# A new order table for a block-sparse attention fused with a gated feed-forward: other engines and buffers for many pieces, three more pairs of score banks, 42 unread products instead of 102

## The chip, the cores and the metric

The kernel runs on one core of a Trainium2 chip. The metric is the device time of that core in microseconds (us). The engines are PE (matrix products; its loading of weights is shown as PEld), DVE (vector), ACT (activations), POOL, also called GpSimd, and SP, which here only issues DMA transfers. [...]

## The reference

Four batches of eight heads, 768 positions and 64 dimensions. Each block of 32 queries sees the blocks beside it, the first and the last block of the sequence, and three sampled blocks; the first and the last block of queries see everything. The result of the attention goes through a gated feed-forward.

```python
batch, n_heads, seq, head_dim = (4, 8, 768, 64)
scores = scale * np.matmul(q, k.transpose(0, 1, 3, 2))
mask = np.abs(blk_i - blk_j) <= window
mask = mask | (blk_i == 0) | (blk_j == 0) | (blk_i == n_blocks - 1) | (blk_j == n_blocks - 1)
# and the three sampled blocks of each block of queries
attn = softmax(np.where(mask, scores, -1e9)); x = np.matmul(attn, v)
gate = 1.0 / (1.0 + np.exp(-(x @ w_gate)))     # 512 -> 1536
return (gate * (x @ w_val)) @ w_out            # 1536 -> 512
```

## The kernel before

The work is cut into 1446 named pieces, each some instructions on one engine. A table, ORDER, lists them in one row: for each piece its name, its engine (P, A, D, G, S for PE, ACT, DVE, GpSimd and SP), the number of each buffer that it takes, and after a plus sign how many unread products of 128x512 (tile WZ, line 1083) PE does ahead of it. `Planner.run` walks the table and the pieces are issued in that order, so every engine's queue is a part of the table. The lines that set it:

```python
item, _, idle = item.partition("+")
name, _, how = item.partition(":")
o.eng, o.idle = self.ENG[how[0]], int(idle or 0)
...
for o in pl.run(ORDER):
    for _ in range(o.idle):
        pin(nc.tensor.matmul(banks[7], WZ[:, 0:128], WZ, start=True, stop=True))
```

The names in the table, with the batch first (`sl0_81` is batch 0, the step that begins with block 8, half 1):

- `ldk`, `ldq`, `ldv`: the loads of a batch (DMA issued by GpSimd, line 417). `trk`, `trq`, `evk`, `evq`: transposition of K and Q on PE and its copy out of PSUM (tiles KT and QT). `vsh`: V put into another order (line 587, tile XL or stg). `scr`: V written back to DRAM. `w`: a window of four blocks of V read from there into V1, `vg`: the three sampled blocks of V of one block read into V2 (SP, line 745), `vfl`: the first and last block copied in (line 641).
- Each batch has eleven steps of two blocks. `kw` copies the window of K (line 728), `kg` gathers three sampled blocks of K for each of two blocks on GpSimd (line 712, six copies), `kfl` the fixed ones. `sc`: scores on PE into a pair of banks (lines 784 and 773); `mx`: row maxima on DVE (line 796); `ex`: exponentials with sums on ACT, one piece for each half of the heads (line 806, tile P, three buffers); `rz`: reciprocal of the sums (line 815); `sl`: the multiplication of P with it, one piece for each half, on ACT (line 828, two instructions), DVE (line 830, two instructions) or GpSimd (line 824, one instruction); `tp`: transposition on PE (line 842); `te`: copy out of PSUM (line 848, tile PTS, three buffers); `pv`: product with V (line 860); `xe`: copy into the feed-forward's input (lines 887 and 889, tiles XT and XL).
- `dsc`, `dmx`, `dex`, `dsl`, `dtp`, `dte`, `dpv`, `dxe` are the same for the first and the last block of queries, which see all keys (lines 916 to 996).
- The feed-forward works on nine groups of rows (128 rows in groups 0 and 1, 256 in 2 to 4, 512 in 5 to 8) and twelve slices of the width 1536: `pg` and `pu`: the gate's and the value's products (line 1029), `th`: tanh on ACT (line 1038), `h`: the gating on DVE (line 1043, tile HT), then for each 128 rows `py`: the output product (line 1060, twelve products), `ys`: copy (DVE line 1067, ACT line 1069), `st`: store.

Banks: scores take a pair out of banks 0, 1 and 2; banks 3 and 4 take the transpositions and the attention's products; banks 5, 6 and 7 take the feed-forward's products (group 0 has 5 and 6 alone, the last two groups take all eight). The first four steps may also have the pair of banks 5 and 6. The pairs come from one line:

```python
spool = duo((0, 1), (1, 2), (0, 2), *TUNE["sx"])
```

Of the kernel before, what the change touches and what calls it, by code (L numbers as in the profile page):

```python
# [17 lines left out]
B, H, S, D = 4, 8, 768, 64  # L18
# [27 lines left out]
 'sx': [],  # L46
# [10 lines left out]
vg0_5:S dte0_00:D regPOOL0_1:G ex0_60:A2 dtp0_01:P0+4 vg0_7:S rz0_4:D sl0_41:D ex0_61:A sc0_8:P0 sc0_10:P3 kw0_14:D2
sl0_40:A rz0_6:D mx0_8:D7 vg0_4:S kw0_12:A1 tp0_4:P11+3 dte0_01:A mx0_10:D1 kg0_12:G vg0_6:S sl0_60:A dpv0_0:P0+4
w0_8:G0 sl0_61:D ex0_80:A1 te0_4:D wv1:G vg0_8:S ex0_81:A sc0_12:P2+2 tp0_6:P10 kw0_18:G1 ex0_100:A0 vg0_11:S
kg0_14:G te0_6:D ex0_101:A mx0_12:D0 pv0_4:P1+3 wg2:G vg0_9:S kg0_18:G rz0_8:D rz0_10:D ex0_120:A2 xe0_4:D dxe0_0:D  # L60
vg0_10:S sl0_100:A sl0_80:G pv0_6:P0+8 sl0_101:A sc0_14:P0 wv2:G xe0_6:D kw0_2:A2 sl0_81:D w0_12:G0 pg0_0:P00+2
pu0_0:P1 th0_0:A0 tp0_10:P12 h0_0:D kw0_16:D0 pg0_1:P10 regSP0_1:S mx0_14:D1 pu0_1:P0 kg0_16:G th0_1:A2 tp0_8:P00
ex0_121:A pg0_2:P10 h0_1:D wo0:G te0_10:D pu0_2:P0+1 th0_2:A2 ex0_140:A0 pg0_3:P10 vg0_13:S h0_2:D regPOOL0_2:G
rz0_12:D sl0_120:D pu0_3:P0 th0_3:A0 sl0_121:A pg0_4:P10+1 h0_3:D te0_8:D pu0_4:P0 th0_4:A2 vg0_12:S ex0_141:A
sc0_16:P2 h0_4:D pg0_5:P10 mx0_16:D5 pv0_8:P1 kw0_20:A0 pu0_5:P0 w0_16:S0 tp0_12:P00 th0_5:A1 kg0_20:G ex0_160:A1
h0_5:D vg0_15:S rz0_14:D sl0_141:D pg0_6:P00+1 pu0_6:P1 te0_12:D th0_6:A0 w0_2:G0 xe0_8:A sc0_18:P0 h0_6:D pg0_7:P00
mx0_18:D4 pu0_7:P1 ex0_161:A pv0_10:P0 vg0_14:S wo1:G th0_7:A1 ex0_180:A2 h0_7:D pg0_8:P00+2 rz0_16:D xe0_10:D
kg0_2:G th0_8:A2 vg0_19:S sl0_160:D pu0_8:P0+3 pg0_9:P10 kw0_1:G1 sl0_161:D sc0_2:P2 h0_8:D th0_9:A1 ex0_181:A wo2:G
pu0_9:P0 mx0_2:D7 vg0_18:S pg0_10:P10 tp0_16:P02 kg0_1:G th0_10:A0 pu0_10:P1 h0_9:D ex0_20:A1 pg0_11:P00 h0_10:D
sl0_140:G vg0_16:S pu0_11:P1 th0_11:A1 ex0_21:A sc0_20:P0+1 h0_11:D vfl0A:G pg1_0:P10 mx0_20:D3 pu1_0:P0 th1_0:A0  # L70
pg1_1:P20 pu1_1:P1 th1_1:A2 tp0_14:P11 te0_16:A h1_0:D h1_1:D pg1_2:P00 rz0_18:D sl0_181:D pu1_2:P1 ldv10:G0
vg0_17:S pg1_3:P20 th1_2:A2 rz0_2:D pv0_12:P0 h1_2:D th1_3:A0 sl0_20:G pu1_3:P2 xe0_12:A pg1_4:P10 h1_3:D te0_14:D
regSP0_2:S pu1_4:P2 w0_1:G0 th1_4:A0 ex0_200:A0 pg1_5:P10 h1_4:D sl0_180:D pu1_5:P0 pg1_6:P20 sl0_21:D th1_5:A2
pv0_14:P0 th1_6:A0 h1_5:D ldk10:G1 pu1_6:P2 vg0_3:S xe0_14:A pg1_7:P10 h1_6:D pu1_7:P0 ldq10:G2 pg1_8:P20 th1_7:A2
sc0_1:P2 h1_7:D th1_8:A0 vfl0B:G ex0_201:A pu1_8:P1 vg0_21:S mx0_1:D2 pg1_9:P00 tp0_18:P10 th1_9:A2 pu1_9:P2
pg1_10:P00 h1_8:D rz0_20:D tp0_2:P01 h1_9:D vg0_20:S th1_10:A0 sl0_201:D ex0_10:A2 pu1_10:P2 pg1_11:P10 h1_10:D
pu1_11:P2 th1_11:A0 sl0_200:A dsc0_23:P02 h1_11:D ex0_11:A py1_0:P2 dmx0_231:D1 vg0_2:S rz0_1:D dmx0_230:D4
dex0_231:A0 dex0_230:A1 dsl0_231:D py0_0:P1 sl0_11:D te0_2:A ys1_0:D0 dsl0_230:D te0_18:A vsh1:D3 dtp0_230:P00
# [12 lines left out]
sc1_6:P0 ys2_0:A1 py2_1:P1 kg1_8:G rz1_20:D mx1_6:D3 te1_2:A st2_0:S vg1_20:S kw1_10:G0 sl1_201:A sl1_200:D ldq20:G0
rz1_4:D h3_0:D ex1_60:A1 sl1_40:D kg1_10:G regSP1_0:S pg3_1:P20 ex1_61:A sc1_8:P2 pv1_1:P1 mx1_8:D7 kw1_12:G1
ys2_1:A0 tp1_20:P02 regPOOL1_1:G th3_1:A2 pu3_1:P1 sl1_41:A w1_4:S0 rz1_6:D te1_20:D pg3_2:P20 ex1_80:A2 vg1_7:S
pu3_2:P0 xe1_1:D tp1_4:P00 th3_2:A1 sl1_60:G ex1_81:A sc1_10:P0 h3_1:D vg1_6:S h3_2:D pg3_3:P10 mx1_10:D5 kg1_12:G
te1_4:A pu3_3:P0 pg3_4:P20 th3_3:A2 vg1_4:S kw1_14:G0 pv1_2:P0 th3_4:A0 h3_3:D ex1_100:A0 kg1_14:G pu3_4:P1 xe1_2:D
pg3_5:P00 pu3_5:P2 rz1_8:D h3_4:D th3_5:A2 sl1_61:A sc1_12:P2 h3_5:D pg3_6:P10 kw1_16:G1 mx1_12:D0 ex1_101:A
tp1_6:P11 vg1_5:S pu3_6:P0 th3_6:A2 sl1_81:D ex1_120:A1 pg3_7:P10 h3_6:D pv1_20:P0 rz1_10:D te1_6:D sl1_101:G
th3_7:A0 pu3_7:P2 w1_8:S0 xe1_20:A dsc1_0:P02 h3_7:D vg1_11:S sl1_80:G ex1_121:A dmx1_01:D1 pg3_8:P20 th3_8:A2
kg1_16:G dmx1_00:D2 dex1_01:A0 pu3_8:P2 scr2:S tp1_8:P12 h3_8:D dex1_00:A1 pg3_9:P10 dsl1_01:D pu3_9:P2 th3_9:A0
dsl1_00:D te1_8:A dsc1_23:P02 h3_9:D dtp1_00:P00 dmx1_231:D7 dtp1_01:P1 vg1_8:S pg3_10:P20 dte1_00:D dex1_231:A0  # L100
dte1_01:D pv1_4:P0 th3_10:A2 pu3_10:P0 dmx1_230:D1 vg1_9:S xe1_4:A dpv1_0:P1 sl1_100:D dex1_230:A1 h3_10:D
tp1_10:P00 vg1_10:S rz1_12:D pg3_11:P20 dxe1_0:A dsl1_230:D pu3_11:P1 te1_10:A dsl1_231:D dtp1_230:P10 w2_2:S0
sc1_14:P0 th3_11:A0 dte1_230:D dtp1_231:P0 kw1_18:G0 h3_11:D pv1_6:P1 kg1_18:G mx1_14:D4 dte1_231:A py3_0:P1
w1_12:S0 xe1_6:A gv2:S sl1_121:D ex1_140:A0 st2_1:S regSP1_1:S ex1_141:A dpv1_23:P1 ys3_0:A1 rz1_14:D pv1_8:P0
dxe1_23:D rrq2:G3 sc1_16:P2 vg1_13:S pg4_0:P10 mx1_16:D1 pv1_10:P1 th4_0:A2 py3_1:P2 sl1_120:A sl1_140:G vg1_14:S
xe1_10:D ex1_160:A2 sl1_141:G xe1_8:A st3_0:S ex1_161:A w1_16:S0 pu4_0:P0 vg1_19:S trk201:P1 h4_0:D pg4_1:P10
# [1009 lines left out]
```

## Time and profile before

| | |
|---|---|
| median of 3 runs | 339.71 us (338.84 to 340.23) |
| span of the profiled execution, first to last instruction | 336.5 us |
| the profiled execution's own time | not among the times listed; the median is 3.2 us above the span |
| busy: PE, DVE, ACT, GpSimd | 318.1, 230.8, 232.4, 128.1 us |
| unread products (line 1083) | 102, busy 28.5 us |
| DMA | 43.14 MB, mean 128 GB/s |

An engine's busy time is the union of its instructions, whose ends are modelled on PE, so a busy PE is not at its peak. "x4" behind a row stands for four instructions. What stands in square brackets behind a row is the idle time ahead of it and the engine that ended it. The granted clock is a share of TensorE's full clock.

### The profile page before, as it was taken

What the parts mean: (1) busy time and instruction counts of PE and PEld (TensorE: products, weight loads), DVE (VectorE), ACT (ScalarE), POOL (GpSimd) and SP (SyncE); (2) the same over time, 40 slices, a digit from 0 to 9 for tenths busy, and PEclk for the clock granted to TensorE, in tenths of its full rate; (3) what the DMA queues carried; (4) which work ended last, traced back from release to release, by engine and by line L of the source; (5) the groups of instructions that cost most, each with busy time, mean ns of one, the idle gap of its engine ahead of it and who ended that gap; (6) DMA issues with size and microseconds to landing.
All of it is one profiled execution on the core that took longest, in us unless ns stands there. A gap on an engine that the chain in (4) does not pass through costs nothing.

```text
span 336.5 us, 11685 instructions
## 1 busy us (share of the span) xinstructions
PE 318.1 (95%) x4230; PEld 194.5 (58%) x4230; DVE 230.8 (69%) x493; ACT 232.4 (69%) x663; POOL 128.1 (38%) x376
## 2 busy tenths in 40 slices
PE   8999887899999789999998999999999999999995
PEld 3545565748776667796555655555645555554442
DVE  3677787777888896697878687698986855423330
ACT  1759785782789887866886788898999764523320
POOL 6575774614777433353184414522522100000000
PEclk9999997999999999999999999999999999999999
DMA  7999999986976655476984344241242352011002
GB/s 115 206 233 216 179 260 209 181 155 186 150 168 100 162 171 157 133 116 129 216 162 125 92 123 134 69 132 33 51 130 70 108 150 52 7 57 64 0 31 94
DMA packets 42873, 43.14 MB, mean 128 GB/s; under 512 B 6560, under 2 KB 39200, under 8 KB 42720
## 3 DMA queue, kind: packets, MB, share of 16 engines
q0 software_dynamic: 14736, 15.93, 29.5%
q1 hardware_dynamic: 28080, 26.47, 27.0%
q8 instruction: 33, 0.54, 0.7%
q14 instruction: 24, 0.20, 0.2%
HBM read 47.10 MB, written 9.44 MB: 168 GB/s over the span
## 4 chain that ended last, share of the span: by engine, by line
PE 70%; DMA 8%; DVE 8%; ACT 7%; issue 3%; POOL 2%; SPq 1%; POOLq 0%; DVEq 0%; ACTq 0%
PE pall L1029 32%; PE pall L1060 17%; PE pall L860 6%; PE pall L842 4%; DMA stg<-in_v_dram 4%; ACT P L806 4%; PE pall L784 3%; PE pall L551 2%; PE pall L970 2%; DVE HT L1043 2%; DMA V2C<-scr 2%; DMA scr<-XL 2%; ACT TH L1038 2%; PE pall L950 1%; DVE NM L796 1%
## 5 line engine op out<-in xcount | busy, mean ns | idle before, releaser
L1038 ACT ACTIVATE TH<-pall 128x512 f32<-128x512 f32 (+2 forms) x108 | 49.1, 459 | 54.7 <-PE pall L1029 46.7
L806 ACT ACTIVATE P<-pall,NM 128x256 f16<-128x256 f32 x176 | 81.3, 477 | 6.5 <-DVE NM L796 5.7
L1043 DVE SCALAR_TENSOR_TENSOR HT<-TH,pall 128x512 f16<-128x512 f32 (+2 forms) x108 | 53.6, 506 | 33.3 <-PE pall L1029 27.3
L1060 PE MATMUL pall<-wo,HT 128*128 128x512 f16 x288 | 65.5, 379 | 0.2 <-DVE HT L1043 0.2
L796 DVE TENSOR_REDUCE NM<-pall 128x4 f32<-128x1024 f32 x44 | 53.6, 1220 | 14.5 <-PE pall L773 9.7
L712 POOL COPY KG<-KT 128x64 f32 x264 | 53.0, 251 | 24.8 <-PE pall L773 18.4
L1029 PE MATMUL pall<-XT,wv 128*128 128x256 f16 (+2 forms) x336 | 56.1, 290 | 4.4 <-DVE HT L1043 3.7
L1029 PE MATMUL pall<-XT,wg 128*128 128x256 f16 (+2 forms) x336 | 56.0, 290 | 3.7 <-DVE HT L1043 1.9
L1029 PEld LDWEIGHTS <-wg 128*128 128x128 f16 x432 | 37.8, 98 | 28.9 <-issue 8.2
L1029 PEld LDWEIGHTS <-wv 128*128 128x128 f16 x432 | 37.8, 99 | 26.7 <-issue 7.3
L1060 PEld LDWEIGHTS <-HT 128*128 128x128 f16 x288 | 26.9, 98 | 32.0 <-issue 1.2
L806 ACT ACTIVATION_READ_ACCUMULATOR P<-pall,NM 128x1 f32 x176 | 36.8, 209 | 0.0
L824 POOL TENSOR_TENSOR P<-P,ZZ 128x512 f16<-128x512 f16 x19 | 19.6, 1039 | 31.8 <-DVE ZZ L815 12.9
L1083 PE MATMUL pall<-WZ 128*128 128x512 f16 x102 | 28.5, 414 | 1.2 <-DVE WZ L371 1.2
L828 ACT ACTIVATE P<-P,ZZ 128x256 f16<-128x256 f16 x54 | 24.4, 514 | 4.7 <-DVE ZZ L815 4.7
L842 PE MATMUL pall<-ident,P 128*128 128x128 f16 x352 | 26.9, 219 | 0.1
L842 PEld LDWEIGHTS <-P 128*128 128x128 f16 x352 | 22.1, 98 | 5.1 <-issue 1.5
L1029 PE MATMUL pall<-XL,wg 128*128 128x512 f16 x96 | 24.0, 379 | 0.0
L1029 PE MATMUL pall<-XL,wv 128*128 128x512 f16 x96 | 24.0, 379 | 0.0
L848 ACT COPY PTS<-pall 128x1024 f16<-128x1024 f16 x21 | 21.2, 1016 | 3.7 <-PE pall L842 3.6
L830 DVE TENSOR_SCALAR P<-P,ZZ 128x256 f16<-128x256 f16 x84 | 23.2, 330 | 0.6
L784 PE MATMUL pall<-KG,QT 64*32 64x256 f16 x704 | 18.8, 277 | 1.2 <-ACT P L806 0.8
(106 smaller groups left out, 448.1 us busy)
## 6 DMA issues: line engine op xcount, KB each, us to landing
out_dram<-YS SPq DMA_DIRECT2D x24, 256.0 KB, 2.0
stg<-in_q_dram POOLq DMA_DIRECT2D x4, 768.0 KB, 9.7
stg<-in_v_dram POOLq DMA_DIRECT2D x4, 768.0 KB, 8.7
V2C<-scr SPq DMA_DIRECT2D x96, 32.0 KB, 2.7
V2D<-scr SPq DMA_DIRECT2D x78, 32.0 KB, 2.6
stg<-in_k_dram POOLq DMA_DIRECT2D x3, 768.0 KB, 8.6
scr<-stg SPq DMA_DIRECT2D x12, 192.0 KB
wg<-in_moe_w_gate_dram POOLq DMA_DIRECT2D x3, 512.0 KB, 8.0
```

The lines of the kernel that those rows point to most:

```text
L712: pin(nc.gpsimd.tensor_copy(t[:, :, u, KO[r] + (2 + n) * BLK : KO[r] + (3 + n) * BLK].bitcast(f32), KT[r].bitcast(f32)[:, :, bass.ds(regs[ ...
L784: pin(nc.tensor.matmul(t[32 * p : 32 * p + 32, hh, u * 256 + c0 : u * 256 + c1], QT[r][kp, p, i * BLK : (i + 1) * BLK], src, start=(merged ...
L796: pin(nc.vector.tensor_reduce(NM[o.slots[hz][1]][:, 0:4].rearrange("p (h u) -> p h u", h=2), t, axis=AX.X, op=ALU.max, negate=True))
L806: pin(nc.scalar.activation(pb[:, hh, u, :], t[:, hh, u * 256 : u * 256 + 256], AF.Exp, bias=NM[z][:, 2 * hh + u : 2 * hh + u + 1], scale=1 ...
L828: pin(nc.scalar.activation(pb[:, u, :], pb[:, u, :], AF.Copy, scale=z[:, 2 * hh + u : 2 * hh + u + 1]))
L830: pin(nc.vector.tensor_scalar(pb[:, u, :], in0=pb[:, u, :], scalar1=z[:, 2 * hh + u : 2 * hh + u + 1], scalar2=None, op0=ALU.mult))
L842: pin(nc.tensor.transpose(t[:, m * 128 : m * 128 + 128], pb[:, hh, u, c * 128 : c * 128 + 128], ident))
L1029: pin(nc.tensor.matmul(t, wt[:, c, f_ * 128 : f_ * 128 + 128], XT[g][:, c, :], start=(c == 0), stop=(c == 3)))
L1038: pin(nc.scalar.activation(TH[o.slots[ht][1]][:, 0:n], banks[pl.handles[hg][1]][:, 0:n], AF.Tanh, bias=0.0, scale=0.5))
L1043: pin(nc.vector.scalar_tensor_tensor(HT[:, f_, hoff : hoff + n], in0=TH[pl.handles[ht][1]][:, 0:n], scalar=1.0, in1=banks[pl.handles[hv][1 ...
L1060: pin(nc.tensor.matmul(t, HT[:, f_, hoff + tt * 128 : hoff + tt * 128 + 128], wo[:, f_, :], start=(f_ == 0), stop=(f_ == NF - 1)))
L1083: pin(nc.tensor.matmul(banks[7], WZ[:, 0:128], WZ, start=True, stop=True))
```

## The change

ORDER is another table: the same 1446 pieces in another order, many on another engine or in another buffer. TUNE gets three more pairs of banks for scores, each with bank 5.

```diff
- 'sx': [],
+ 'sx': [(0, 5), (1, 5), (2, 5)],
...
-trq001:P0+13 kfl00:G trq002:P2 evq001:A kfl01:G trq000:P1 evq002:D regPOOL0_0:G evq000:A trq003:P2+3 evq003:A
-kg0_8:G dsc0_0:P12+4 vsh0:D0 kg0_6:G dmx0_01:D1 scr0:S dmx0_00:D3 dex0_01:A0 kg0_4:G regSP0_0:S dex0_00:A1 dsl0_01:D
...
+trk002:P2+2 trk003:P3 trq001:P1+11 evk002:A trq000:P0 evq000:A memset:G mask:D vfl0A:D evk003:D evq001:D trq002:P2
+evq002:D trq003:P3 evq003:A dsc0_0:P02 dmx0_00:D0 vfl0C:G dmx0_01:D1 vsh0:D0 kw0_8:A1 regSP0_0:S scr0:S w0_4:S0
```

The unread products: before, 23 ahead of the first transposition, 68 more up to the first product of the feed-forward, 11 behind that. Now 16, 26 and none; the last three stand ahead of the score of step 14 of batch 0.

Pieces by engine, where they differ most:

| piece | before | now |
|---|---|---|
| `sl` (88 halves) | ACT 27, DVE 42, GpSimd 19 | ACT 5, DVE 34, GpSimd 49 |
| `te` (44) | ACT 21, DVE 23 | ACT 12, DVE 32 |
| `xe` (44) | ACT 17, DVE 27 | ACT 31, DVE 13 |
| `kw` (44) | ACT 14, DVE 13, GpSimd 17 | ACT 8, DVE 12, GpSimd 24 |
| `ys` (24) | ACT 18, DVE 6 | ACT 13, DVE 11 |
| `w` (24) | GpSimd 5, SP 19 | GpSimd 1, SP 23 |

The two halves of a step's `sl` are on DVE and GpSimd in 25 of the 44 steps (8 before), both on GpSimd in 10 (3 before), on ACT and DVE in 1 (18 before).

The line numbers of the kernel after are 2 lower, since the table is two lines shorter.

GpSimd's queue at the start of the program, before (V1D and V2D are the pads of a V window, KG the gathered K, wg and wv weights):

```order
L431 DMA wg<-in_moe_w_gate_dram 128x4x512
L431 DMA wv<-in_moe_w_val_dram 128x4x512
L641 COPY V1D<-GV 32x1024
L641 COPY V2D<-GV 32x1024
L655 COPY KG_93<-KT_74 128x4x32 x2
L655 COPY KG_91<-KT_74 128x4x32 x2
L655 COPY KG_92<-KT_74 128x4x32 x2
L453 TENSOR_LOAD kidx
```

The same place now:

```order
L639 COPY V1C<-GV 32x1024
L639 COPY V2C<-GV 32x1024
L639 COPY V1D<-GV 32x1024
L639 COPY V2D<-GV 32x1024
L429 DMA wv<-in_moe_w_val_dram 128x4x512
L429 DMA wg<-in_moe_w_gate_dram 128x4x512
L451 TENSOR_LOAD kidx
L429 DMA wv<-in_moe_w_val_dram 128x4x512
L429 DMA wg<-in_moe_w_gate_dram 128x4x512
L653 COPY KG_93<-KT_74 128x4x32 x2
```

Both pads of window C moved from DVE to GpSimd, and the loads of weights, which stood between the later steps' gathers, now stand ahead of the first gather.

GpSimd's queue in batch 1, around steps 6 to 10, before (P0 and P2 are the buffers of the exponentials, ZZ their sums; the rows are the last gather of one step, a copy of K's window and `sl1_101` and `sl1_80`):

```order
L712 COPY KG10_94<-KT1_75 128x4x16
L728 COPY KG11_95<-KT1_75 128x8x48
L824 TENSOR_TENSOR P0_96<-P0_96,ZZ5_112 128x512
L824 TENSOR_TENSOR P2_98<-P2_98,ZZ7_114 128x512
L712 ISA
```

Now (`sl1_60`, `sl1_81`, a load, a copy of K's window, `sl1_80`, `sl1_100`):

```order
L710 COPY KG10_94<-KT1_75 128x4x16
L822 TENSOR_TENSOR P0_96<-P0_96,ZZ2_109 128x512
L822 TENSOR_TENSOR P2_98<-P2_98,ZZ1_108 128x512
L415 DMA stg0_78<-in_q_dram 96x8x512
L726 COPY KG10_94<-KT1_75 128x8x48
L822 TENSOR_TENSOR P2_98<-P2_98,ZZ1_108 128x512
L822 TENSOR_TENSOR P1_97<-P1_97,ZZ6_113 128x512
```

Four multiplications of steps 6 to 10 stand here instead of two.

DVE's queue in the same place, now (rows of `rz1_10`, `sl1_101`, two `h`, `rz1_12`, two `dmx`, `evk201`, an `h`, and `dsl1_01`):

```order
L813 RECIPROCAL ZZ6_113<-ZZ6_113 128x4
L828 TENSOR_SCALAR P1_97<-P1_97,ZZ6_113 128x256 x2
L1041 SCALAR_TENSOR_TENSOR HT_73<-TH0_121,pall_64 128x256
L1041 SCALAR_TENSOR_TENSOR HT_73<-TH2_123,pall_64 128x256
L813 RECIPROCAL ZZ4_111<-ZZ4_111 128x4
L925 TENSOR_REDUCE NM2_101<-pall_64 128x1
L925 TENSOR_REDUCE NM3_102<-pall_64 128x1
L569 COPY KT0_74<-pall_64 128x768
L1041 SCALAR_TENSOR_TENSOR HT_73<-TH1_122,pall_64 128x256
L939 RECIPROCAL ZZ2_109<-ZZ2_109 128x1
L940 TENSOR_SCALAR DP1_119<-DP1_119,ZZ2_109 128x768
```

The other half of step 10 (`sl1_100`, P1 with ZZ6) is the last GpSimd row above, so DVE and GpSimd work on one buffer's two halves behind the same reciprocal.

More of the change, by code (lines that the diff above doesn't have):

```diff
@@ L57 @@
[L57 to L66, printed above, removed]
@@ L102 @@
[L102 to L106, printed above, removed]
@@ L167 @@
[L167 to L170 removed]
+wz:D ldk00:G0 ldk01:G ldq00:G1 ldv00:G2 cdma:S wg0:G trk000:P2+16 evk000:A idx:D gv0:S gc0:D trk001:P1 evk001:A
@@ L171 @@
+py8_2:P4 ys8_2:A0 st8_2:S
 """
```

215 lines of the change are left out of this document (113 added, 102 removed).

## The prediction

> **What bounds the kernel now.** I read the busy time by stages first, with cuts at the first product of the feed-forward (38.41 us), at 80, 97.5 and 129.65 us and at the last product. The columns are start and end, length, then busy time and instructions of PE, PEld, DVE, ACT and POOL, the granted clock, the busy share of the DMA engines and GB/s. Below the six rows stand two of the same view with the unread products (line 1083) alone, where the columns are PE and PEld only.
>
> ```profile
> 0.00:38.41 38.41, 35.41 (x477) 17.57 (x478) 24.20 (x53) 23.79 (x61) 26.22 (x79) 1.00 1.03 190
> 38.41:80.10 41.69, 35.65 (x594) 26.26 (x592) 33.40 (x81) 27.48 (x96) 21.45 (x41) 0.96 1.03 203
> 80.10:97.50 17.40, 17.30 (x294) 14.64 (x291) 13.67 (x33) 13.54 (x42) 9.95 (x35) 1.00 0.91 173
> 97.50:129.65 32.15, 29.11 (x491) 21.27 (x489) 27.06 (x59) 28.15 (x85) 17.32 (x51) 1.00 0.54 127
> 129.65:332.84 203.19, 200.61 (x2384) 114.75 (x2382) 132.45 (x269) 138.84 (x381) 53.22 (x174) 1.00 0.38 99
> 332.84:336.50 3.66, 0.00 (x0) 0.00 (x0) 0.00 (x0) 0.60 (x1) 0.00 (x0) 1.00 0.19 72
> 0.00:38.41 38.41, 25.28 (x93) 8.76 (x93) 1.00 1.03 190
> 38.41:80.10 41.69, 3.19 (x10) 0.82 (x9) 0.96 1.03 203
> ```
>
> Behind 129.65 PE is free for only 203.19 - 200.61 = 2.58 us: a better order can win almost nothing there, since PE's own products are the same in both tables. Up to 38.41 PE is nearly always busy, but 25.28 of its 35.41 us are products that nobody reads, so something else sets this stretch. From 38.41 to 80.10 PE lacks 6.04 us, while DVE is busy for 80% of it; from 97.50 to 129.65 it lacks 3.04, with DVE and ACT at 84% and 88%. The change can move the time in the first 130 us.
>
> What sets the first 38 us is read in the chain that ended last (start, length, what):
>
> ```profile
> 4.55 13.67 DMA stg<-in_v_dram
> ...
> 19.50 5.67 DMA scr<-XL
> ...
> 30.78 6.03 DMA V2C<-scr
> 36.85 0.61 PE pall L860 x15
> ```
>
> Batch 0's V is loaded, put in order by DVE, written back and read again block by block; the product with V follows and the feed-forward behind it. No transposition or score is in this chain. The longest wait behind it comes from DVE. First the waits that I use (total, times, longest), then PE around the largest one, with its idle time in brackets, and PE's busy time and clock in three windows (length, PE busy, clock, DMA share, GB/s):
>
> ```profile
> PE pall L1029 <- DVE HT L1043: 5.6, 7, 2.4
> PEld L784 <- ACT P L806: 2.4, 4, 0.9
> ```
>
> ```profile
> 53.44 0.38 PE L1029 MATMUL pall<-XT,wv 128*128 128x128 f16 x4 [2.41 <-DVE HT L1043]
> 57.50 0.55 PE L1029 MATMUL pall<-XT,wv 128*128 128x128 f16 x4
> 58.11 0.39 PE L1029 MATMUL pall<-XT,wv 128*128 128x128 f16 x4
> ```
>
> ```profile
> 33.93:37.35 3.42, 2.44 (x26) 1.00 1.00 162
> 51.00:54.42 3.42, 1.01 (x25) 1.00 1.21 204
> 54.42:57.83 3.41, 3.39 (x47) 0.50 1.22 219
> ```
>
> Why DVE was late at 53 us is read in the timelines of DVE and POOL. The rows are three places: 50 us; 174 us; and, for comparison, 150, 237 and 242 us.
>
> ```profile
> 50.00 3.06 DVE L830 TENSOR_SCALAR P<-P,ZZ 128x256 f16<-128x256 f16 x4
> 50.58 1.03 POOL L824 TENSOR_TENSOR P<-P,ZZ 128x512 f16<-128x512 f16 x1
> 51.67 1.12 POOL L641 COPY V1A<-GV 32x1024 f32<-32x1024 f32 x1
> 174.53 2.03 DVE L728 COPY KG<-KT 128x768 f16<-128x768 f16 x1
> 173.57 3.43 POOL L712 COPY KG<-KT 128x64 f32 x18
> 150.00 0.48 DVE L830 TENSOR_SCALAR P<-P,ZZ 128x256 f16<-128x256 f16 x2
> 237.19 0.87 DVE L830 TENSOR_SCALAR P<-P,ZZ 128x256 f16<-128x256 f16 x4
> 236.81 1.52 POOL L712 COPY KG<-KT 128x64 f32 x8
> 241.93 1.26 DVE L830 TENSOR_SCALAR P<-P,ZZ 128x256 f16<-128x256 f16 x2
> 242.04 1.07 POOL L824 TENSOR_TENSOR P<-P,ZZ 128x512 f16<-128x512 f16 x1 [1.81 <-DVE ZZ L815]
> ```
>
> A pair of `sl` instructions takes DVE 0.48 us alone and 1.26 beside a GpSimd `sl`: 1.26 - 0.48 = 0.78 more, nearly the other's length. Four behind one another beside two long GpSimd instructions took 3.06 instead of 0.96, 2.10 more, and this is the 2.41 us for which PE stood, after which the clock was halved. Four beside eight short copies took 0.87: those do no harm one by one, but a row of 18 held one copy of K for 2.03 us. [...]
>
> **The change, part by part.** Durations of the pieces, from the groups by line and shape (busy, mean ns, idle ahead):
>
> ```profile
> L828 ACT ACTIVATE P<-P,ZZ 128x256 f16<-128x256 f16 x54 | 24.4, 514 | 4.7 <-DVE ZZ L815 4.7
> L830 DVE TENSOR_SCALAR P<-P,ZZ 128x256 f16<-128x256 f16 x84 | 23.2, 330 | 0.6
> L824 POOL TENSOR_TENSOR P<-P,ZZ 128x512 f16<-128x512 f16 x19 | 19.6, 1039 | 31.8 <-DVE ZZ L815 12.9 <-PE pall L1029 6.7 <-PE pall L784 5.8
> L848 ACT COPY PTS<-pall 128x1024 f16<-128x1024 f16 x21 | 21.2, 1016 | 3.7 <-PE pall L842 3.6
> L848 DVE COPY PTS<-pall 128x1024 f16<-128x1024 f16 x23 | 15.6, 680 | 2.8 <-PE pall L842 2.8
> L889 DVE CAST XT<-pall 64x256 f16<-64x256 f32 x18 | 7.5, 419 | 4.0 <-PE pall L860 3.9
> L796 DVE TENSOR_REDUCE NM<-pall 128x4 f32<-128x1024 f32 x44 | 53.6, 1220 | 14.5 <-PE pall L773 9.7 <-ACT P L806 2.8 <-PE pall L1029 1.2
> ```
>
> *Relief of DVE up to the first output product of group 3* (129.65 us before). Counted in the table, DVE's list there loses 2 halves of `sl` (23.2/42 = 0.55 each) and 6 `xe` (two casts, 0.84), and gains 4 `te` (0.68) and one `mx` (1.22); its other changes cancel. -1.10 - 5.03 + 2.72 + 1.22 = -2.2 us. DVE and PE wait for one another there, so I count it whole; the bounds are 0 and the 6.0 that PE lacks from 38 to 80. ACT loses more over the whole program (22 halves at 0.90 = 19.9 less, and 9 `te` at 1.02 less, 14 `xe` more), but most lies behind 129.65.
>
> *The rest.* Behind 129.65 PE had 2.58 us free; I take -1.0 (0 to -2.6).
>
> *Three more pairs of banks.* Scores wait 2.4 us for exponentials to leave their bank (the row above). Half of it goes: -1.2 (0 to -2.4). The other half lies where the feed-forward holds bank 5.
>
> *GpSimd beside DVE.* GpSimd gets 30 more halves of `sl`, 30 x 1.04 = 31 us of work where the stages show it free. But in the table a fast DVE piece stands within two places ahead of or four behind a GpSimd `sl` (eight for a copy into V's pads) 28 times; before, 3 times. Of the 28, 15 lie ahead of py3_0; 6 of these come before the first product of the feed-forward, hidden by the wait for V. So 9 x 0.78, of which three quarters really meet: 5.3, less the 2.1 at 50.00 that goes: +3.2. Behind it 13 x 0.78 x 3/4 = 7.6, of which PE's queue of ready products hides 60%: 3.0, less the 1.5 at 174.53 (2.03 against the 0.50 of a copy of K in this row) that goes: +1.5.
>
> ```profile
> L728 DVE COPY KG<-KT 128x768 f16<-128x768 f16 x13 | 6.5, 500 | 1.3 <-PE pall L773 1.1
> ```
>
> Together +4.7. Bounds: no meeting at all, -3.6; all 22 in full, 17.2 - 3.6 = +13.6.
>
> *Fewer unread products.* None now stands between the score of step 14 and the product with V of step 4, about 27 to 36 us, where PE's own work is thin (10.1 us in the first 38). At 25.28/93 = 0.27 each, 51 fewer up to 38 us leave 13.9 us more idle. A window with 1.01 us busy was followed by half the clock, one with 2.44 was not, so I expect half the clock as the feed-forward begins. There a quartet takes 0.55 instead of 0.39 us: 3.4 us of work until the clock is back cost 1.4, and the pieces just ahead of it some 0.6. +2.0, between 0 (DVE sets the pace anyway) and +4 (twice as long). The unread products themselves lay in PE's waits: nothing.
>
> *The chain of V.* SP now reads window 4 ahead of the sampled blocks, and these in the order 4, 6, 5, 7 instead of 5, 7, 4, 6; both weights stand ahead of the gathers on GpSimd's DMA queue. Other transfers already stretch the V load to 13.67 and the last gather to 6.03 us. One more window in front of the reads is some 0.7: +0.7 (-1 to +3, half of that last transfer).
>
> The sum is made against the profiled span: -2.2 - 1.0 - 1.2 + 4.7 + 2.0 + 0.7 = +3.0, 336.5 + 3.0 = 339.5 us. The profiled execution's own time is not listed; the median stands 3.2 above its span, so the time is **342.7 us**. About 0.5%, 1.7 us, is what a measurement of this kernel can tell from no change.
>
> **The rivals.**
>
> *Faster: the meetings do not hurt.* Neighbours in a table need not meet on the clock: DVE's half may be done before GpSimd starts, as both begin behind one reciprocal but GpSimd often has a gather in front (5.8 of its idle time ahead of `sl` ended with a score, not the reciprocal). Then DVE's relief stays and the two stalls of before go: -2.2 - 1.0 - 1.2 - 3.6 + 0.7 + 1.0 for the clock = -6.3, 330.2 of span, **333.4 us**. For it: idle GpSimd, DVE and ACT both lighter. Against: 242 us shows the very pair that the new table has 25 times. It decides at about 5 us of delay less on the path, some seven meetings.
>
> *Slower: the clock stays low from 27 to 75 us.* With 10 unread products gone there and DVE late, PE's windows are again thin several times. [...] The dip here followed a longest wait of 2.41. Two dips more than the forecast has, each 3.4 us at 0.55/0.39, 1.4, with DVE's work behind them late by as much again: +3 to +5, **345 to 347**. Against it: the clock's mean from 38 to 80 us was 0.96 with only 3.19 us of unread products there.
>
> *Slower: bank 5 is taken from the feed-forward.* Eleven scores of batches 1 to 3 hold it for about 3 us each (maxima 1.22 and exponentials); if a quarter hits a product that is due, +3 us on the rest of the sum, **345.7**. Against it: the planner's order places them, and banks 6 and 7 remain.
>
> *A wash.* The chain of V and PE's products stay as they are, and relief and delays cancel: 338.0 to 341.4.
>
> **How the numbers follow.** Forecast 0.34, own range 340.5 to 346; meetings harmless 0.33; clock 0.12; bank 5 0.06; wash 0.15. Faster by over 0.5% is the second case, 0.33; the same, 0.15; slower 0.34 + 0.12 + 0.06 = 0.52. As both signs have much of the chance, the range takes in the faster case with 1.4 us below its middle for a larger relief, 332.0, and the clock's upper end with 1 us for meetings that all hurt, 348.0; a tenth is left outside on either side.
>
> **What would show it.** Right: DVE's `sl` with a mean well over 330 ns and pairs above 1 us beside GpSimd's; half the clock in a window between 31 and 45 us; the first product of the feed-forward at about 39; its waits for HT above 5.6 us; PE free for no more than 2.6 us behind the third group's first output product. Wrong: `sl` pairs on DVE at 0.5 us although GpSimd works on the other half; waits for HT below 4 us; first output product of group 3 before 127 us, which is the faster case; or a first product of the feed-forward before 37 us, since then the chain of V was shortened, which I hold unlikely.

## The result and the profile after

The kernel after takes 357.14 us (median of 4, 353.33 to 360.75) against 339.27 (median of 4): 1.052 times before, 95% interval 1.043 to 1.061. It is 17.9 us slower; forecast were 3.0 us slower, and the range ended at 348. Its profiled execution took 355.86 us with a span of 354.1, so 1.8 us lie around the span, not the 3.2 that I had taken. Medians in this document are over all executions; ratios leave out those that took over 1.5% longer than the fastest of their kernel.

The stages, cut at the same pieces as before (`pg0_0`, group 0 and slice 0, the first product of the feed-forward; `pg2_0`; `pg3_0`; `py3_0`, the first output product of group 3; the last product), with the columns as before:

```profile
0.00:47.17 47.17, 32.59 (x459) 16.87 (x459) 29.28 (x57) 24.02 (x66) 33.95 (x89) 0.78 1.13 207
47.17:81.15 33.98, 28.84 (x497) 23.38 (x494) 25.33 (x62) 22.29 (x83) 17.34 (x33) 0.91 0.67 145
81.15:103.50 22.35, 21.07 (x352) 16.98 (x351) 16.05 (x32) 15.71 (x43) 10.49 (x34) 1.00 0.60 146
103.50:137.45 33.95, 30.26 (x531) 22.48 (x529) 30.39 (x61) 26.04 (x85) 21.59 (x58) 1.00 0.74 169
137.45:350.30 212.85, 200.30 (x2347) 115.66 (x2345) 132.68 (x245) 126.52 (x361) 72.33 (x196) 1.00 0.34 90
```

The loss shows in two places. The first product of the feed-forward comes 8.8 us later (47.17 against 38.41), and the first output product of group 3 is 7.8 us late (137.45 against 129.65). The cut between them at `pg2_0` is only 1.1 us late, but says little: before, the output products of both first groups stood ahead of it, now one of the two. At `pg3_0` the delay is 6.0 us. And behind the first output product of group 3, where PE had been free for 2.58 us, it is now free for 212.85 - 200.30 = 12.55, about 10 us more. DVE and ACT are no busier there than before (132.68 and 126.52 us against 132.45 and 138.84).

The first loss in the chain that ended last:

```profile
20.66 1.14 DVE XL L585
21.82 7.90 DMA scr<-XL
29.74 7.43 DMA V1C<-scr
...
40.66 8.01 DMA V1D<-scr
...
51.14 4.74 DMA V2D<-scr
```

It is still the chain of V, but V's write takes 7.90 us instead of 5.67, and two windows of V stand in it with 7.43 and 8.01 us, which were not in it before. Between the two windows stands SP: it issued V1C at 29.74 us and seven small reads behind it, stopped at 33.6, went on at 37.19, as V1C had landed, and came to V1D at 40.66.

The second loss in PE's waits (total, times, longest):

```profile
PE pall L840 <- DVE NM L794: 8.0, 7, 2.0
PE pall L858 <- DMA V2C<-scr: 4.8, 3, 3.8
PE pall L1027 <- DVE HT L1041: 3.7, 7, 0.9
...
PE pall L948 <- DVE NM L794: 1.2, 1, 1.2
PE pall L968 <- DVE NM L794: 0.9, 1, 0.9
```

The waits for HT, on which I had put DVE's delays, fell from 5.6 to 3.7. New are waits of transpositions (line 840) for NM, the maxima of scores, of which they use nothing. One of them, first on PE, then on DVE:

```profile
113.27 0.44 PE L840 MATMUL pall<-ident,P 128*128 128x128 f16 x5 [1.89 <-DVE NM L794]
```

```profile
110.86 2.36 DVE L794 TENSOR_REDUCE NM<-pall 128x4 f32<-128x1024 f32 x2 [0.39 <-PE pall L771]
```

This is `tp1_20`. Its two multiplications were done at 109.94 us and its bank had been read out at 109.55; it started when the second of the two maxima, `mx1_8`, ended. That score has the pair of banks 1 and 5. All nine of PE's waits for maxima in these rows are of this kind: each ends as the maximum of a score in a pair with bank 5 ends, three in batch 0 (`mx0_6`, `mx0_10`, `mx0_14`; 4.6 us), this one, and five behind 137.45 us (`mx2_20`, `mx2_8`, `mx3_1`, `mx3_2`, `mx3_4`; 3.5 us).

### The profile page after: what moved, and what is told of

The parts are those of the page before. It is cut to its first block, busy times and chain, and to the rows that moved or that the text cites. A ratio compares the mean times of both kernels' runs of the same rounds, so it can differ in the third digit from the quotient of the medians.

```text
span 354.1 us, 11525 instructions
## 1 busy us (share of the span) xinstructions
PE 313.1 (88%) x4170; PEld 195.4 (55%) x4170; DVE 233.7 (66%) x453; ACT 215.2 (61%) x637; POOL 155.7 (44%) x407
## 4 chain that ended last, share of the span: by engine, by line
PE 55%; DVE 18%; DMA 12%; ACT 7%; issue 6%; SPq 2%; DVEq 0%; ACTq 0%
PE pall L1027 27%; PE pall L1058 12%; DVE NM L794 6%; PE pall L858 4%; PE pall L840 4%; ACT P L804 4%; DMA V2D<-scr 3%; DVE P L828 3%; DMA V1D<-scr 2%; DVE HT L1041 2%; DMA scr<-XL 2%; PE pall L549 2%; DMA V1C<-scr 2%; PE pall L782 2%; DMA HT<-in_v_dram 1%
## 5 line engine op out<-in xcount | busy, mean ns | idle before, releaser
L822 POOL TENSOR_TENSOR P<-P,ZZ 128x512 f16<-128x512 f16 x49 | 51.0, 1048 | 84.2 <-DVE ZZ L813 76.5
L1036 ACT ACTIVATE TH<-pall 128x512 f32<-128x512 f32 (+2 forms) x108 | 48.7, 460 | 36.1 <-PE pall L1027 27.8
L710 POOL COPY KG<-KT 128x64 f32 x264 | 52.2, 248 | 3.3 <-issue 2.0
L840 PE MATMUL pall<-ident,P 128*128 128x128 f16 x352 | 28.0, 225 | 8.0 <-DVE NM L794 8.0
L840 PEld LDWEIGHTS <-P 128*128 128x128 f16 x352 | 23.4, 101 | 14.3 <-issue 9.8
L828 DVE TENSOR_SCALAR P<-P,ZZ 128x256 f16<-128x256 f16 x68 | 27.7, 455 | 0.7
L726 POOL COPY KG<-KT 128x384 f32<-128x384 f32 (+1 forms) x27 | 12.5, 470 | 30.0 <-PE pall L771 21.8
L846 DVE COPY PTS<-pall 128x1024 f16<-128x1024 f16 x32 | 21.8, 683 | 2.6 <-PE pall L840 2.2
L782 PE MATMUL pall<-KG,QT 64*32 64x256 f16 x704 | 20.3, 291 | 3.5 <-ACT P L804 1.8
L1067 ACT ACTIVATE YS<-pall 128x512 f32<-128x512 f32 x13 | 7.8, 599 | 24.1 <-PE pall L1058 22.0
## 6 DMA issues: line engine op xcount, KB each, us to landing
stg<-in_v_dram POOLq DMA_DIRECT2D x4, 768.0 KB, 10.3
```

The lines of the kernel that those rows point to most:

```text
L710: pin(nc.gpsimd.tensor_copy(t[:, :, u, KO[r] + (2 + n) * BLK : KO[r] + (3 + n) * BLK].bitcast(f32), KT[r].bitcast(f32)[:, :, bass.ds(regs[ ...
L782: pin(nc.tensor.matmul(t[32 * p : 32 * p + 32, hh, u * 256 + c0 : u * 256 + c1], QT[r][kp, p, i * BLK : (i + 1) * BLK], src, start=(merged ...
L822: pin(nc.gpsimd.tensor_tensor(pb, pb, z[:, 2 * hh : 2 * hh + 2].unsqueeze(2).broadcast_to([128, 2, 256]), op=ALU.mult))
L828: pin(nc.vector.tensor_scalar(pb[:, u, :], in0=pb[:, u, :], scalar1=z[:, 2 * hh + u : 2 * hh + u + 1], scalar2=None, op0=ALU.mult))
L840: pin(nc.tensor.transpose(t[:, m * 128 : m * 128 + 128], pb[:, hh, u, c * 128 : c * 128 + 128], ident))
L846: pin(copy(o)(PTS[pl.handles[hTS][1]].rearrange("p m n -> p (m n)"), banks[pl.handles[hT][1]].bitcast(f16)))
```

## The experiments

### The banks renumbered

```diff
-    banks = [pall[:, i, :] for i in range(8)]
+    AT = (0, 1, 2, 6, 7, 3, 4, 5)
+    banks = [pall[:, i, :] for i in AT]
 def pair(h):
-    a, b = (s[1] for s in pl.whole[h])
+    a, b = sorted(AT[s[1]] for s in pl.whole[h])
     return pall[:, a : b + 1 : b - a, :]
```

> The kernel after with its eight banks renumbered and nothing else: what the table calls banks 3, 4, 5, 6, 7 are the physical banks 6, 7, 3, 4, 5. A score in a pair with bank 5 then spans banks 0 to 3 and no longer steps over the two banks of the transpositions. Theory A (the strided view of such a pair is tracked as one stretch, so transpositions wait for the maxima and exponentials of a score that they have nothing to do with): PE's waits for the maxima (8.0 us at the transpositions, 1.2 and 0.9 at those of the dense blocks in the kernel after) fall below 2 us and the time falls by 5 to 9 us, to 348 to 352. Theory B (the transpositions waited for their own operands, late since GpSimd and DVE hold each other up): the waits stay and the time stays within 2 us of 357.

347.40 us (346.07 to 350.1), 1.028 times before (1.020 to 1.036): 9.7 us faster than the kernel after, a little more than expected, with every piece, engine and queue as it was. All that is left of the transpositions' waits:

```profile
PE pall L840 <- POOL KG L710: 0.4, 1, 0.4
PE pall L840 <- DVE P L828: 0.3, 1, 0.3
```

DVE's multiplications were no shorter for it, with a mean of 518 ns:

```profile
L828 DVE TENSOR_SCALAR P<-P,ZZ 128x256 f16<-128x256 f16 x68 | 31.8, 518 | 0.7
```

Theory A holds: the pair with bank 5 is one strided view, from bank `a` to bank `b`; between 0, 1 or 2 and 5 lie banks 3 and 4, those of the transpositions, and PE waited 8.0 us there for the view's readers, the maxima, where no wait for them is left in these rows now. The gain lies behind the first output product of group 3, which comes at 137.15 us here (137.45 in the kernel after): from there to the last product PE is free for 205.35 - 199.65 = 5.70 us instead of 12.55. Of those 6.85 us the waits for maxima make up 3.5; the others, shorter waits of products and scores behind them, were not taken apart. The waits in batch 0 went too, but there the first product of the feed-forward waited for V all the same (46.82 us). That the tracking takes the view as one stretch is argued from the code; that the waits hang on the bank numbers alone is shown (8.0 us with the old numbers, none with the new).

### Windows of V on GpSimd again

```diff
-... scr0:S w0_4:S0 vg0_4:S ... vg0_7:S w0_8:S0 ... w0_12:S0 ...
+... kg0_12:G w0_4:G0 kg0_14:G ... kg0_18:G w0_8:G0 wo2:G ldv10:G1 ldk10:G3 ldq10:G0 w0_12:G0 ...
```

> The kernel after with the first three windows of V of batch 0 issued by GpSimd, as before the change, instead of SP. Theory C (SP's queue has eight transfers in flight at most, so a window that takes 7 to 8 us to land stops the reads of the sampled blocks behind it, at 33.3 to 37.2 and 45.5 to 48.7 us in the kernel after): the stops go, the first product of the feed-forward comes at 40 to 43 us instead of 47.2, and the time falls by 4 to 6 us. Theory D (the DMA engines are full between 20 and 60 us, whoever issues): the first product stays at 46 to 48 and the time within 2 us.

359.90 us (359.8 to 360.24), 1.068 times before (1.060 to 1.077), no gain; the first product came at 47.8. SP issued the first twelve sampled reads in 6.3 us instead of 10.3, but the window now landed 13.1 us after its issue (last column), against 4.5 in the kernel before. First this kernel's row of issues, then the row of before:

```profile
V1C<-scr POOLq DMA_DIRECT2D x1, 384.0 KB, 13.1
```

```profile
V1C<-scr POOLq DMA_DIRECT2D x1, 384.0 KB, 4.5
```

In the trace GpSimd had issued eight loads of weights ahead of this window, before the change three. So theory C's stops, which the trace of the kernel after shows (eight transfers out by 33.6 us and none until the first had landed at 37.2; eight more by 45.8 and none until 48.7), are not what this time hangs on; but the edit took the window from SP's queue only to put it behind the weights, and what the stops cost by themselves stays open.

### The loads of batch 1 later

```diff
-... wo2:G ldv10:G1 ldk10:G3 ldq10:G0 ex0_120:A1 ...
+... wo2:G ex0_120:A1 ... sl0_161:G ldv10:G1 ldk10:G3 ldq10:G0 ...
```

> The kernel after with the three loads of batch 1 issued some 17 us later (behind the second GpSimd multiplication of step 16 of batch 0), so that they don't run beside the reads of V of batch 0. Theory D (full DMA engines): the first product of the feed-forward comes 2 to 4 us earlier and the time falls by 2 to 4 us. Theory C (the queue of eight): the windows land somewhat earlier, the first product by 0 to 1 us, the time by 0 to 1.

356.41 us (352.73 to 363.89), 1.058 times before (1.046 to 1.069): within the spread of the kernel after. The first product stayed at 47.1, so these loads are not the ones in the way of V's first windows. The first output product of all came 3.7 us earlier (73.04 us against 76.78); in the median little of this was left.

### The multiplications on their former engines

```diff
-... sl0_41:D sl0_40:G ...
+... sl0_41:D sl0_40:A ...
```

So for 70 of the 88 halves.

> The kernel after with every half of the multiplication (sl) on the engine that it had before the change: 27 on ACT, 42 on DVE, 19 on GpSimd. The order stays. Theory E (DVE stuck beside GpSimd, as forecast): DVE's excess in these instructions falls from 11.4 to about 4 us, and the time by 4 to 8 us. Rival F (these delays were covered; the time is set by the start and by false waits): the time stays within 2 us, or rises by up to 4 since ACT gets 20 us of work more.

364.41 us (359.34 to 366.47), 1.071 times before (1.057 to 1.086): slower by 5 to 7 us than the kernel after, more than either theory had expected. DVE's rows (busy, mean ns) show that the delays beside GpSimd did go, from a mean of 455 to 320 ns. The first fence is the kernel after, the second this one:

```profile
L828 DVE TENSOR_SCALAR P<-P,ZZ 128x256 f16<-128x256 f16 x68 | 27.7, 455 | 0.7
```

```profile
L827 DVE TENSOR_SCALAR P<-P,ZZ 128x256 f16<-128x256 f16 x84 | 23.0, 320 | 0.4
L825 ACT ACTIVATE P<-P,ZZ 128x256 f16<-128x256 f16 x54 | 24.1, 507 | 5.7 <-DVE ZZ L812 5.6
```

But ACT, which had 10 such instructions in the kernel after, has 54 again, and PE's transpositions wait for it:

```profile
PE pall L839 <- ACT P L825: 3.9, 2, 2.6
```

The order had been made for GpSimd's help; what the meetings cost in it can't be read from this run.

### Later weights

```diff
-... wg1:G regPOOL0_0:G wv1:G wg2:G ... wv2:G ... kg0_4:G ... wo0:G ... wo1:G ...
+... wg1:G regPOOL0_0:G ... kg0_14:G wv1:G ... kg0_18:G wg2:G wv2:G wo0:G wo1:G wo2:G ...
```

> The kernel after with six of its nine loads of weights (wv1, wg2, wv2, and the three of w_out, 512 KB each) issued later, as before the change: wv1 behind the gather of step 14, the others behind that of step 18. Theory D, sharpened (the transfers are served in the order of their issue by full DMA engines, and the kernel after puts five more weights of 512 KB, 13 us of transfer at some 200 GB/s, ahead of V's write and reads): V's write lands in under 6.5 us instead of 7.9, the first window in under 6 instead of 7.4, the first product of the feed-forward comes at 40 to 43 us instead of 47.2, and the time falls by 3 to 6 us. Theory C (SP's eight transfers in flight) alone: the first product stays at 46 to 47.

Five loads move; the sixth, `wo2`, stood behind the gather of step 18 already. The first product came 7.2 us earlier:

```profile
39.93 0.39 PE L1026 MATMUL pall<-XT,wg 128*128 128x128 f16 x4
```

The time, though, was 355.83 us (351.71 to 357.14), 1.044 times before (1.034 to 1.055), 1.3 us less than the kernel after, which is within the spread of the two and not the 3 to 6 expected. In its trace the gain is 3.9 us at the first output product of all (72.90 us against 76.78), 3.4 at the first product of group 3 and 1.1 at the first output product of that group. Between the first two of these PE now waits for the sampled blocks of another window (V2B, 3.1 us in all), and the false waits are all there still (transpositions 7.4 us), those of batch 0 and `tp1_20` among them.

### The multiplications of the kernel after, in the kernel before

```diff
-... sl0_41:D ... sl0_40:A ...
+... sl0_41:D ... sl0_40:G ...
```

Again 70 halves, now the other way.

> The kernel before with the multiplications (sl) alone on the engines of the kernel after: 5 on ACT, 34 on DVE, 49 on GpSimd. Theory E (DVE stuck beside GpSimd costs time on the path, as forecast): slower by 3 to 8 us, 342 to 347, with DVE's excess in these instructions up from 3.9 to over 10 us. Rival F (the delays are covered, GpSimd's help is free): within 1.5 us of before, or up to 3 us faster since DVE and ACT have less to do.

343.81 us (341.22 to 344.49), 1.011 times before (1.002 to 1.019): slower by 5.4 us by the medians, by 3.6 by the ratio. That is of the size that the forecast gave to this term (+4.7), but not in its place: the first output product of group 3 comes 0.7 us later (130.36 against 129.65), where 3.2 were forecast, and the rest lies behind it, spread over the stretch from 160 to 260 us, where 1.5 were. The waits for HT rose from 5.6 to 5.9 us only. New are waits of transpositions for the half that GpSimd does itself:

```profile
PE pall L839 <- POOL P L821: 1.8, 4, 0.7
```

So this run shows what the engines cost, and not that DVE's delays are the cause: a late GpSimd half, which the forecast had not named, has a part in it.

### More unread products

```diff
-... sc0_12:P0+1 ... tp0_6:P01 ... tp0_8:P12 ... pv0_4:P0 ... pv0_6:P1 ... pg0_0:P10 ... pv0_8:P0 ... pv0_10:P1 ...
+... sc0_12:P0+3 ... tp0_6:P01+4 ... tp0_8:P12+6 ... pv0_4:P0+14 ... pv0_6:P1+5 ... pg0_0:P10+3 ... pv0_8:P0+2 ... pv0_10:P1+5 ...
```

> The kernel after with 42 more unread products ahead of the scores, transpositions and products with V between 32 and 57 us. Theory G (the clock, halved between 27 and 50 us, costs time there): the granted clock between 27 and 47 us rises from 0.67 to over 0.9, and the time falls by 1 to 3 us. Rival (the stretch waits for V, PE has time enough at half the clock): the clock rises and the time stays within 1 us.

The edit adds 41. The clock between 27 and 47 us, first in the kernel after, then here (length, busy times, clock, DMA share, GB/s):

```profile
27.30:47.20 19.90, 11.82 (x222) 7.87 (x222) 11.58 (x24) 11.76 (x42) 11.49 (x33) 0.67 1.21 224
```

```profile
27.30:47.20 19.90, 17.25 (x271) 10.09 (x248) 12.25 (x25) 12.18 (x45) 11.68 (x35) 0.89 1.21 230
```

The clock rose from 0.67 to 0.89, just short of the 0.9 expected, the last product of group 1 came 3.9 us earlier, and the time stayed: 358.16 us (356.59 to 359.87), 1.057 times before (1.049 to 1.065). As with the weights, the lead was lost again: 2.2 us were left at the first output product of group 3, nothing at the end.

### Banks, weights and loads together

Three of the edits above in one kernel, called the mended kernel from here on:

```diff
+    AT = (0, 1, 2, 6, 7, 3, 4, 5)
+... kg0_14:G wv1:G ... kg0_18:G wg2:G wv2:G wo0:G wo1:G wo2:G ... sl0_161:G ldv10:G1 ldk10:G3 ldq10:G0 ...
```

> The kernel after with three edits at once: the renumbered banks of the first experiment (9.7 us by itself), the late weights, and the late loads of batch 1 (4 us earlier at 72 us by its profile, though the whole time moved little). If theories A and D are the whole of the loss: 9.7 + 4 to 6 + 2 to 4, so 337 to 342 us, level with before. If a part of the loss lies elsewhere: 343 to 347.

342.01 us (340.48 to 344.57), 1.013 times before (1.008 to 1.017): 15.1 of the 17.9 us are gone.

### One meeting taken out of the kernel before

```diff
-... sl0_160:D ... sl0_161:D ... sl0_140:G ... vfl0A:G ... ldv10:G0 ...
+... sl0_160:D ... sl0_161:D sl0_140:D ... ldv10:G0 vfl0A:G ...
```

> The kernel before with one meeting taken away: the half sl0_140 goes from GpSimd to DVE, behind sl0_161, and the copy into V's pad (vfl0A) goes behind the load of V of batch 1. Theory E: DVE's four instructions at 50.0 us take about 1.1 us instead of 3.06, the fifth and sixth 0.55, PE's wait of 2.41 us for HT falls under 1.2, and the time falls by 1 to 2.5 us. Rival F: the stall was covered, or is given back behind it: within 0.7 us.

335.81 us (333.97 to 344.06, 12 executions), 0.993 times before (0.990 to 0.996): faster than both kernels, by little but clear of the interval. DVE does six instructions in 1.48 us where four had taken 3.06, PE waits 0.83 us instead of 2.41, and the clock stays whole where it had been 0.50:

```profile
50.30 1.48 DVE L827 TENSOR_SCALAR P<-P,ZZ 128x256 f16<-128x256 f16 x6
```

```profile
52.15 0.38 PE L1026 MATMUL pall<-XT,wv 128*128 128x128 f16 x4 [0.83 <-DVE HT L1040]
```

```profile
51.00:54.42 3.42, 2.47 (x53) 1.00 1.19 192
54.42:57.83 3.41, 3.41 (x78) 1.00 1.23 220
```

GpSimd, with a half less to do, also issues the load of V of batch 1 3.0 us sooner (50.90 us instead of 53.91); what that is worth by itself was not tried.

### Both halves of 25 steps on DVE

In the mended kernel, in each step that DVE and GpSimd share:

```diff
-... sl0_41:D sl0_40:G ...
+... sl0_41:D sl0_40:D ...
```

> The mended kernel (renumbered banks, late weights, late loads; 342.0 us) with 25 halves of the multiplication moved from GpSimd to DVE, in the 25 steps whose other half DVE has already. Theory E (a DVE half beside a GpSimd half takes 1.1 us, as long as both halves alone): DVE's busy time rises by less than 5 us for 25 pieces more, and the time stays within 1.5 us or falls. Rival F (most halves did not meet, GpSimd's work was free help): DVE is busy 14 us longer and the time rises by 3 to 8 us.

341.92 us (339.44 to 346.83), 1.012 times before (1.006 to 1.019): the same time as without the edit. DVE's and GpSimd's rows, first of the mended kernel, then of this one:

```profile
L822 POOL TENSOR_TENSOR P<-P,ZZ 128x512 f16<-128x512 f16 x49 | 50.7, 1042 | 74.0 <-DVE ZZ L813 69.8 <-ACT TH L1036 3.2 <-ACT KG L726 0.7
L828 DVE TENSOR_SCALAR P<-P,ZZ 128x256 f16<-128x256 f16 x68 | 32.8, 528 | 0.7
```

```profile
L828 DVE TENSOR_SCALAR P<-P,ZZ 128x256 f16<-128x256 f16 x118 | 31.1, 318 | 0.6
L822 POOL TENSOR_TENSOR P<-P,ZZ 128x512 f16<-128x512 f16 x24 | 24.7, 1043 | 58.7 <-DVE ZZ L813 57.1 <-ACT XT L887 0.7 <-ACT KG L726 0.7
```

DVE does 118 instructions in less time (31.1 us) than 68 beside GpSimd's (32.8). The 26.0 us that GpSimd had worked bought nothing: on the whole a shared step cost DVE as much as both halves cost it alone.

### V first and unread products in the mended kernel

```diff
-... dmx0_00:D0 vfl0C:G dmx0_01:D1 vsh0:D0 ... sc0_12:P0+1 ... pv0_4:P0 ... pv0_10:P1 ...
+... vsh0:D0 dmx0_00:D0 vfl0C:G dmx0_01:D1 ... sc0_12:P0+3 ... pv0_4:P0+8 ... pv0_10:P1+5 ...
```

> The mended kernel (342.0 us) with two edits more: V of batch 0 is put in order on DVE ahead of the maxima of the first dense block, not behind them, and 30 unread products stand ahead of the pieces between 32 and 50 us. By theory D the chain of V starts at 17.4 instead of 20.2 us and the first product of the feed-forward comes at 38 to 40 instead of 41.3; by theory G the clock is over 0.9 from 38 to 60 us. Together 339 to 341 us; 338 or less would beat the kernel before.

341.69 us (339.99 to 345.71), 1.011 times before (1.006 to 1.017), 0.3 less than the mended kernel, which is nothing measurable and less than expected. DVE put V in order 2.6 us earlier, from 17.66 instead of 20.25, and the first product came at 40.4 instead of 41.3: with 29 unread products more (42 and 71 in all), little of it arrived. Which part of the chain took the rest was not followed.

### Early weights in the kernel before

```diff
-... vfl0D:G ... kg0_8:G ... kg0_6:G ... wg1:G ... kg0_10:G ... wv1:G ... wg2:G ... wv2:G ... wo0:G ...
+... vfl0D:G wg1:G wv1:G wg2:G ... wv2:G kg0_8:G ... kg0_6:G wo0:G ... kg0_10:G wo1:G ...
```

> The kernel before with its loads of weights issued as early as in the kernel after (wg1, wv1, wg2 behind the first ones, wv2 and two of w_out between the first gathers). Theory D: the first windows of V wait behind 3 MB of weights, land after 38 us instead of 30, the first product of the feed-forward comes at 43 to 47 us instead of 38.4, and the time rises by 3 to 6 us. Rival (the start of the kernel after was late by the order on PE and DVE, not by the weights): the first product stays at 38 to 40 and the time within 1.5 us.

348.00 us (347.45 to 348.54), 1.031 times before (1.026 to 1.036): 9.4 us slower, more than theory D had said, with the first product at 51.07 us. V's first window, and what PE waited for it:

```profile
V1C<-scr POOLq DMA_DIRECT2D x1, 384.0 KB, 17.9
```

```profile
PE pall L857 <- DMA V1C<-scr: 9.9, 1, 9.9
```

Of the two parts of the change that were put into the kernel before, this costs more. It issues its windows of V on GpSimd's queue, behind these loads, and SP's stops at the windows are not in it, so the weights alone suffice for a late V.

### Banks and weights alone

The mended kernel without the late loads:

```diff
-... wo2:G ... sl0_161:G ldv10:G1 ldk10:G3 ldq10:G0 ...
+... wo2:G ldv10:G1 ldk10:G3 ldq10:G0 ... sl0_161:G ...
```

> The kernel after with two edits: renumbered banks (347.4 us alone) and late weights (355.8 alone, against 357.1). If the gain of the late weights was given back to the false waits (with the weights alone the first product came 7.3 us earlier, and the gain shrank from 4 us at 100 us to nothing at the end), it shows in full now: 347.4 less 3 to 5, 342 to 344, so the late loads are worth little in the mended kernel (342.0). If the late loads are what counts, the time is 346 to 348.

341.29 us (340.98 to 342.0), 1.012 times before (1.003 to 1.021): 6.1 us less than with the banks alone. So the gain of the late weights, 1.3 us by themselves, had been given back to the false waits, and the late loads are worth nothing here. The last stage of this kernel, from its first output product of group 3 to the last product:

```profile
131.00:336.40 205.40, 199.74 (x2348) 115.40 (x2345) 133.49 (x245) 126.25 (x361) 72.05 (x196) 1.00 0.35 97
```

PE is free there for 5.66 us, 3.1 more than in the kernel before.

### All edits

The mended kernel with the edits of the two kernels derived from it:

```diff
-... dmx0_00:D0 ... vsh0:D0 ... pv0_4:P0 ... sl0_41:D sl0_40:G ...
+... vsh0:D0 dmx0_00:D0 ... pv0_4:P0+8 ... sl0_41:D sl0_40:D ...
```

> The kernel after with every edit that helped in a profile: renumbered banks, late weights, late loads, V in order ahead of the dense maxima, 30 unread products, and both halves of the 25 split steps on DVE. By sum 340 to 342 us, since the last two edits moved the mended kernel's 342.0 by 0.3 and 0.1 us; if the fillers and the unblocked DVE add up only together (both shorten the stretch up to 70 us), 336 to 339, level with the kernel before or better.

346.78 us (345.9 to 347.99), 1.028 times before (1.018 to 1.038): 5 us slower than with fewer edits, against both expectations. At 126.9 us its first output product of group 3 was ahead of the kernel before; then PE stood for 9.31 us:

```profile
152.53 0.21 PE L858 MATMUL pall<-PTS,V2D 128*128 128x64 f16 x1 [9.31 <-DMA V2D<-scr]
```

### Two pieces back on GpSimd, ahead of the loads

```diff
-... sl1_161:D ... sl1_140:D ... ldv30:G1 ... ldk30:G0 ...
+... sl1_161:G ... sl1_140:G ... ldv30:G1 ... ldk30:G0 ...
```

> The kernel with all edits (346.8 us) with two of its 25 moved halves back on GpSimd, sl1_161 and sl1_140, which stand ahead of the loads of batch 3 there. In the kernel with all edits GpSimd, freed of them, issued those loads at 139.8 and 141.9 us, ahead of SP's reads of V for step 12 of batch 1 at 142.5, and PE waited 9.3 us for one of these reads. Theory D (transfers served in the order of their issue): with the two halves back GpSimd reaches the loads at 143 us or later, the wait of 9.3 falls under 2 us, and the time falls by 6 to 9 us, to 338 to 341. Rival (the reads were late for SP's own eight transfers in flight): the wait stays above 6 us and the time within 2 us of 346.8.

341.00 us (337.48 to 345.29), 0.999 times before (0.995 to 1.004): 5.8 us less, level with before. The loads, first in the kernel with all edits, then here, and PE's waits for these reads here:

```profile
139.83 0.81 POOL L415 DMA_DIRECT2D stg<-in_v_dram  x1
```

```profile
143.22 0.82 POOL L415 DMA_DIRECT2D stg<-in_v_dram  x1
...
PE pall L858 <- DMA V2D<-scr: 3.8, 3, 2.4
```

The load of V that had gone out at 139.83 us, ahead of the reads of V that SP issued from 142.5 there, goes out at 143.22 here. The expected fall of the wait to under 2 us was missed by a little (2.4).

## Why the prediction was wrong

It had the sign, and missed the size by 14.9 us. The sign was mostly luck: it came from +4.7 for GpSimd beside DVE and +2.0 for the clock, which in the new order were worth nothing that the runs could find, while the loss came from a term forecast as a gain (-1.2) and one of +0.7. Step by step:

- *Three more pairs of banks, -1.2*: the step that failed most. I priced what the pairs give and, as a rival, what they take from the feed-forward's products; neither is what happened. With the pairs' views clear of banks 3 and 4 the kernel is 9.7 us faster; what remained of the -1.2 was not measured. The line that makes the view was printed in the part on the kernel; I read which banks it gives and not what lies between them. The bound "0 to -2.4" excluded a loss without a reason.
- *The chain of V, +0.7 (-1 to +3)*: the mechanism was named (weights ahead of the reads in the DMA queue), the size was off by ten. The first product came 8.8 us later. I had taken one window's worth; five loads more stood ahead, 2.6 MB, and at the 207 GB/s of this stage's row that is, by estimate, some 12.7 us of transfer. Worth 6.1 us where the banks are right, 9.4 in the kernel before.
- *GpSimd beside DVE, +4.7*: right about DVE, wrong about the path. The mean rose from 330 to 455 ns, and one meeting removed from the kernel before gave 0.7%. The new engines in the order of before cost 3.6 to 5.4 us, most of it behind 160 us and not where the term was put, and a late half on GpSimd is a part of it. But in the new order neither removing the meetings with ACT's help (5 to 7 us slower) nor with DVE's (0) won anything, and the renumbered kernel, with a mean of 518 ns, was 9.7 us faster: there these delays were mostly off the path.
- *The rest, -1.0*: the bounds "0 to -2.6" took it that this stretch can only win, and gave no reason. PE became free for 10 us more there. The banks account for 6.9 of them (12.55 to 5.70); why the last 3.1 stay is open.
- *Fewer unread products, +2.0*: the clock fell as forecast (0.67 from 27 to 47 us, 1.00 before). Restored, it gave 3.9 us at 72 us and nothing at the end (with V first in the mended kernel 0.3), so the term was 0 here, inside its bounds.
- *Relief of DVE, -2.2*: not isolated by a run.

Of the signs that I had named, two came as forecast (DVE's multiplications well over 330 ns, half the clock between 31 and 45 us: 0.50 from 42 to 45) and three did not: the first product at about 39 us (47.17), waits for HT above 5.6 (3.7), and PE free for no more than 2.6 us in the last stage (12.55). Waits for HT below 4 us had even been named as a sign of a faster kernel. The two that failed by far, the first product and PE's free time, point at the two steps that failed.

The two mis-sized steps explain 9.7 + 6.1 = 15.8 of the 17.9 us (the banks alone, then the weights on top). The kernel with both edits still lacks about 4 us: 1.4 at its first output product of group 3 (131.03 us against 129.65) and 3.1 of PE's free time behind it. Their cause is not shown; the edits to the clock, to V's order and to GpSimd's halves together, with the loads of batch 3 held back, made it level with before.

## What to carry to other kernels

When a change lends a buffer, list what the view in between touches, since a wait can come from what the view spans and not from the data (8.0 us of PE's waits here). When a planner moves work off a queue, look at the big transfers behind it: issued earlier, they went ahead of the reads that the path needed here (9.4 us of the time at the start, a wait of 9.31 in the middle). And a gain at one stage is only a gain if the next stage has no wait that swallows it: the same edit gave 1.3 us or 6.1.

## What was not expected of the hardware

A load of 384 KB issued by GpSimd landed after 4.5, 13.1 or 17.9 us, with three, eight and eight loads of 512 KB issued ahead of it (in the last it was issued 3.7 us sooner than in the second, at 26.67 us instead of 30.34). Six DVE instructions alone took 1.48 us and four beside two GpSimd instructions 3.06; over a whole kernel, doing 25 halves more took DVE no longer than leaving them to GpSimd (31.1 us against 32.8), so dividing this multiplication between the two engines won nothing (342.01 us against 341.92 with both halves on DVE). And PE's transpositions waited 8.0 us for readers of banks that they do not use, until the banks were renumbered.
